# The pair of buffers in the router's place goes from the first to the fourth chunk of the first expert tile

## The chip, the cores and the metric

The kernel runs on one core of one Trainium2 chip, as one launch. The metric is the device time of that launch in microseconds; lower is better. The names of the engines are those of the profile: PE (TensorE, matrix multiply), PEld (its weight loads), DVE (VectorE), ACT (ScalarE), POOL (GpSimd), SP (the queue that issues most transfers).

## The reference

Three stages follow each other on 2304 tokens of 512 features.

```python
# 1: linear attention, 4 x 8 heads, 576 positions, 64 features per head
q_p, k_p = phi(q), phi(k)             # exp(+-(x @ w_phi - max|.|)), 256 features
attn = (q_p @ (k_p.T @ v)) / (q_p @ sum(k_p) + 1e-6)
# 2: a dense two-layer block on x [2304, 512]
h = x @ w_in                          # [2304, 2048]
x = np.maximum(0.01 * h, h) @ w_out   # [2304, 512]
# 3: each token goes to the one of 8 experts with the largest cosine logit
expert_idx = np.argmax(xn @ en.T / tau, axis=1)
for e in range(8):
    mask = expert_idx == e
    h = np.maximum(x[mask] @ w1[e], 0.0)          # w1[e] [512, 1024]
    out[mask] = gate_w[mask, None] * (h @ w2[e])  # w2[e] [1024, 512]
```

## The kernel before, in words

**Dense block.** Tokens go in 9 blocks of 256. The dense block's hidden features go in 16 chunks; the weights of a chunk are a tile `W` of high and low float32r parts. A first pass over the blocks uses chunks 0 to 7, a second pass (the loop `for j in range(NBLK)`) chunks 8 to 15, which lie in `ring_b`, a pool of eight such tiles. In the second pass `mm1(j, c)` (L344 to L346) forms a chunk of the hidden layer in a PSUM tile `h`; ACT and DVE make the leaky ReLU of it (L349, L351); ACT and POOL split it into `gg` (L353, L355); `mm2(j, c)` (L366) multiplies it by the second weight matrix, two chunks behind. `y_half_b(j)` then adds the two passes (L606), stores the block, and for blocks 0 to 7 takes the product of each token with each of the 8 expert embeddings on DVE (L615, 16 operations per block, all reading the tile `enb`).

**Expert tiles.** The tokens are sorted into tiles of 128 with one expert each; 23 tiles are always run. The list of the first five is made from the first 12 token tiles while the dense block still runs. A tile needs four weight chunks of [128, 2048] from `ew`: chunks 0 and 1 are the halves of w1, chunks 2 and 3 the halves of w2. POOL gathers chunk c into `raw[c]`; `split(c)` makes a high part `whi` (ACT, L921) and a low part `wlo` (DVE, L922), each in two operations over 1024 columns. The pair (`whi`, `wlo`) of each chunk stays where `first_split(c)` put it for the rest of the kernel; later tiles split into the same pair, and skip that if the expert is the same (branches, L932 and L935).

**Where the pairs lie.** `ring_c` has two tiles of [128, 2048] and opens, for the last block, in the place of the pool `lg`, which holds `enb`: what is written there first waits for the last L615 of block 7. `ring_b` gives its eight tiles in turn: the first pair has the place of `W` for dense chunks 8 and 9, the second of 10 and 11, the third of 12 and 13, each to be had after the last `mm2` that reads them.

**Work around the change.** PE's order is written out by hand there (`manual_schedule`), and ACT's too in the first two steps: `up(i, nh)` (12 matmuls with chunk nh, L978 to L982, into a PSUM tile that shares the two buffers of `h`), `hT` (4 transposes, L992, copied out by ACT L995 and DVE L996), `down(i, nh)` (12 matmuls with chunk 2 + nh, L1008 to L1012), `xT` (transposes of the next tile's tokens, L881, copied by L884 and L885). The transposes share a ring of two PSUM buffers `ps_t`. In `step(0)` the order is `up(0,0)`, then `ends()` (the last 12 matmuls of `mm2` of block 8), `hT(0,0)`, `up(0,1)`, `xT(1)`, `hT(0,1)`; in `step(1)` it is `up(1,0)`, `down(0,0)` and so on. All queues run in order. The order on DVE is a scheduler's.

Of the kernel before, what the change touches and what calls it, by code (L numbers as in the profile page):

```python
# [66 lines left out]
def tile_attention_moe_router_experts(ctx, tc, qT, kT, va, w_phi, moew, emb, embT, tau, ew, out):  # L67
# [382 lines left out]
    for j in range(NBLK):  # L450
# [15 lines left out]
        if j == NBLK - 1:  # L466
# [3 lines left out]
            ring_b = ctx.enter_context(tc.tile_pool(name="ring_b", bufs=8, side="left", reuse_waits="tile"))  # L470
# [428 lines left out]
    def load_w(i, c):  # L899
        if i == 0 or i >= N_PLAIN:  # L900
            load_rows(i, c)
            return
        if i not in need:
            need[i] = nc.values_load(
                lists[i][2], engines=[mybir.EngineType.Pool], min_val=0, max_val=4 * NE
            )
        with tc.If(need[i] < NE):
            load_rows(i, c)
# [8 lines left out]
    def split(c):  # L917
        hi, lo = pairs[c]
        for h in range(2):
            hs_ = slice(h * 1024, (h + 1) * 1024)  # L920
            nc.scalar.copy(out=hi[:, hs_], in_=raw[c][:, hs_])  # L921
            nc.vector.tensor_sub(lo[:, hs_], raw[c][:, hs_], hi[:, hs_].bitcast(F32))  # L922

    def first_split(c):
        pool = ring_c if c == 0 else ring_b
        pairs[c] = tuple(pool.tile([P, 2048], F32R, tag="W", name=n) for n in ("whi", "wlo"))
        split(c)
        load_w(1, c)
# [11 lines left out]
    for j in range(NBLK):  # L940
# [3 lines left out]
        if last:  # L944
            lg_cm.__exit__(None, None, None)
            ring_c = ctx.enter_context(tc.tile_pool(name="ring_c", bufs=2, side="right", reuse_waits="tile"))
# [142 lines left out]
    for c in range(4):  # L1089
        first_split(c)  # L1090
# [62 lines left out]
```

## Time and profile before

| | before |
|---|---|
| time, median of 3 runs (lowest to highest) | 927.18 us (926.13 to 929.4) |
| the profiled execution's own time | 925.01 us |
| span of that execution in the profile | 923.3 us |
| PE busy | 881.8 us, 96% of the span |
| DVE, ACT, POOL busy | 60%, 49%, 24% |
| mean granted TensorE clock | 0.984 of full |

The times inside the profile count from the span's start; 1.7 us of the profiled execution's time lie outside the span. A clock of 1.00 in the profile's rows is the upper of TensorE's two levels (2.4 GHz), 0.50 the lower (1.2 GHz). A row of the timeline gives start, duration, engine, line, operation, output and inputs, a count, and in square brackets the idle time ahead of it with what ended it.

### The profile page before, as it was taken

The page shows a single profiled execution, that of the slowest core. Times are in us where ns is not written, and L with a number is a line of the kernel's source. Part 1 is how long each engine was busy: PE and PEld are TensorE (multiplying, and loading weights), DVE is VectorE, ACT ScalarE, POOL GpSimd, SP SyncE. Part 2 cuts the span into 40 slices and gives each one's busy share as a digit, 9 for nine tenths or more (in the row PEclk, how much of TensorE's full clock was granted, in tenths as well). Part 3 has the DMA queues.
Part 4 walks back from the last instruction along what each step waited for, and adds up shares of the span by engine and source line. Part 5 has one row for each costly group of instructions (what it writes and reads, how often), then busy time and mean ns, then how long its engine had stood idle before and what let it go on. Part 6 is the DMA issues. An engine that isn't in the chain of part 4 may idle for free. (4 is left out here: it accounts for less than half of the span.)

```text
span 923.3 us, 18721 instructions
## 1 busy us (share of the span) xinstructions
PE 881.8 (96%) x7104; PEld 757.1 (82%) x7104; DVE 553.2 (60%) x1276; ACT 450.2 (49%) x904; POOL 225.3 (24%) x219
## 2 busy tenths in 40 slices
PE   8979999999999999899999999959999999999994
PEld 6768888889898888788888888838888888888883
DVE  6775557484765554748888899863422761113572
ACT  6965556484745654743333332523423862224571
POOL 2430113031111330033233333501113431113321
PEclk9989999999999999999999999979999999999998
DMA  8873423142130211943222221601014941114570
GB/s 280 290 239 99 133 75 127 50 123 103 48 107 24 104 69 61 324 166 112 86 103 92 98 89 65 240 23 36 28 49 149 351 150 47 41 41 168 183 265 31
DMA packets 42613, 112.36 MB, mean 122 GB/s; under 512 B 4558, under 2 KB 23118, under 8 KB 36496
## 3 DMA queue, kind: packets, MB, share of 16 engines
q1 hardware_dynamic: 33424, 61.48, 20.1%
q0 software_dynamic: 9008, 49.55, 15.4%
q8 instruction: 57, 0.93, 0.4%
q14 instruction: 44, 0.36, 0.1%
q10 hardware_dynamic: 80, 0.03, 0.0%
HBM read 87.45 MB, written 24.90 MB: 122 GB/s over the span
## 5 line engine op out<-in xcount | busy, mean ns | idle before, releaser
L366 PE MATMUL y<-W,gg 128*128 128x512 f32 x864 | 230.0, 400 | 1.0 <-ACT gg L353 1.0
L366 PEld LDWEIGHTS y<-W,gg 128*128 128x128 f32 x864 | 153.0, 189 | 29.0 <-ACT gg L353 1.4
L344 PE MATMUL h<-xb,W 128*128 128x256 f32 x576 | 164.3, 288 | 5.2 <-DVE g L351 3.3
L345 PE MATMUL h<-xb,W 128*128 128x256 f32 x576 | 162.7, 283 | 1.9 <-DVE xb L294 1.6
L346 PE MATMUL h<-xb,W 128*128 128x256 f32 x576 | 162.1, 283 | 0.0
L344 PEld LDWEIGHTS h<-xb,W 128*128 128x128 f32 x576 | 108.1, 189 | 13.3 <-DVE g L351 4.7
L345 PEld LDWEIGHTS h<-xb,W 128*128 128x128 f32 x576 | 108.5, 188 | 7.7 <-DVE xb L294 2.2
L252 POOL PARTITION_ALL_REDUCE qmx<-pr x28 | 56.4, 2016 | 221.6 <-ACT pr L234 218.0
L346 PEld LDWEIGHTS h<-xb,W 128*128 128x128 f32 x576 | 108.5, 189 | 1.6 <-issue 0.2
L353 ACT CAST gg<-g 128x256 fp32r<-128x256 f32 x144 | 57.5, 406 | 96.2 <-DVE g L351 87.5
L615 DVE CUSTOM_DVE_ANT_0 jk<-ys,enb 128x512 f32<-128x512 f32 x128 | 102.5, 801 | 2.0
L349 ACT ACTIVATE t<-h 128x256 f32<-128x256 f32 x144 | 54.5, 382 | 88.4 <-PE h L346 87.7
L351 DVE TENSOR_TENSOR g<-h,t 128x256 f32<-128x256 f32 x144 | 60.1, 420 | 53.4 <-ACT t L349 50.2
L355 POOL TENSOR_TENSOR gg<-g,gg 128x256 fp32r<-128x256 f32 x72 | 59.0, 823 | 134.5 <-ACT gg L353 117.7
L922 DVE TENSOR_TENSOR wlo<-raw,whi 128x1024 fp32r<-128x1024 f32 x56 | 68.1, 1255 | 36.0 <-ACT whi L921 30.3
L996 DVE TENSOR_TENSOR h<-htp,h 128x512 fp32r<-128x512 f32 x46 | 31.7, 689 | 92.9 <-ACTq L935 74.4
L978 PE MATMUL hps<-whi,xt 128*128 128x512 f32 x184 | 77.3, 420 | 9.9 <-ACT whi L921 9.8
L1008 PE MATMUL yo<-whi,h 128*128 128x512 f32 x184 | 74.7, 406 | 0.0
L979 PE MATMUL hps<-wlo,xt 128*128 128x512 f32 x184 | 73.7, 400 | 0.5 <-DVE wlo L922 0.5
L1009 PE MATMUL yo<-wlo,h 128*128 128x512 f32 x184 | 72.6, 395 | 0.0
L921 ACT CAST whi<-raw 128x1024 fp32r<-128x1024 f32 x56 | 55.9, 1047 | 34.2 <-PE hps L982 13.0
L985 ACT ACTIVATE hs<-hps 128x512 f32<-128x512 f32 x46 | 27.4, 595 | 71.3 <-PE hps L982 64.8
(239 smaller groups left out, 1600.0 us busy)
## 6 DMA issues: line engine op xcount, KB each, us to landing
wst<-in_moew_dram SPq DMA_DIRECT2D x32, 512.0 KB, 5.3
qraw<-in_q_dram SPq DMA_DIRECT2D x36, 256.0 KB, 3.0
xs_d<-xb SPq DMA_DIRECT2D x9, 1024.0 KB, 5.4
xb<-xs_d POOLq DMA_DIRECT2D x9, 1024.0 KB, 5.2
kraw<-in_k_dram SPq DMA_DIRECT2D x16, 288.0 KB, 3.3
yp_d<-yt SPq DMA_DIRECT2D x9, 512.0 KB, 3.7
yt<-yp_d SPq DMA_DIRECT2D x9, 512.0 KB, 3.8
y_d<-ys SPq DMA_DIRECT2D x18, 256.0 KB, 2.1
```

The costliest lines, as they stand in the source:

```text
L344: nc.tensor.matmul(hp, w[:, 0, ks], x[:, 0, k, :], start=(k == 0), stop=False)
L345: nc.tensor.matmul(hp, w[:, 0, ks], x[:, 1, k, :], start=False, stop=False)
L346: marks["mm1"] = nc.tensor.matmul(hp, w[:, 1, ks], x[:, 0, k, :], start=False, stop=(k == 3))
L351: nc.vector.tensor_tensor(out=g, in0=hp, in1=t, op=ALU.max)
L355: eng.tensor_sub(gg[:, 1, :], g, gg[:, 0, :].bitcast(F32))
L366: nc.tensor.matmul(yps[j][t], gg[:, a, ts], w[:, b, DM:2 * DM], start=(c0 == 0 and a == 0 and b == 0), stop=(c0 == NCH - 1 and a == 1),)
L615: nc.vector.tensor_tensor_reduce(out=jk2, in0=ys, in1=enb[:, e, :], scale=1.0, scalar=0.0, op0=ALU.mult, op1=ALU.add, accum_out=lgr[:, t, ...
L922: nc.vector.tensor_sub(lo[:, hs_], raw[c][:, hs_], hi[:, hs_].bitcast(F32))
L978: nc.tensor.matmul(ps, x[:, 0, k], hi[:, ks], start=(k == 0), stop=False)
L979: nc.tensor.matmul(ps, x[:, 0, k], lo[:, ks], start=False, stop=False)
L1008: nc.tensor.matmul(yacc[i], h2[:, 0, k], hi[:, w0], start=(nh == 0 and k == 0), stop=False)
L1009: nc.tensor.matmul(yacc[i], h2[:, 0, k], lo[:, w0], start=False, stop=False)
```

## The change

One number decides which chunk's pair comes out of `ring_c`.

```diff
     def first_split(c):
-        pool = ring_c if c == 0 else ring_b
+        pool = ring_c if c == 3 else ring_b
         pairs[c] = tuple(pool.tile([P, 2048], F32R, tag="W", name=n) for n in ("whi", "wlo"))
         split(c)
         load_w(1, c)
```

The four calls still come in the order c = 0, 1, 2, 3. Before, chunk 0 took `ring_c` and chunks 1, 2, 3 the first, second and third pair of `ring_b`; now chunks 0, 1, 2 take those three pairs and chunk 3 takes `ring_c`. No instruction is added or left out but branches of the control flow. The order moves on ACT, DVE and PE.

On ACT, around the last two `gg` of the dense block (`gg_8075`, `gg_8101`) and the first result of `up`, `hs_8179`; `raw0` to `raw3` are the chunks' raw weights, `whi_8110` the high part of chunk 0. Before:

```order
L353 CAST gg_8101<-g_8099 128x256 [waits DVE_49]
L907 UNCONDITIONAL_BRANCH
L921 CAST whi_8110<-raw0_5447 128x1024 [waits DMAHW1_49,DMASW1_49,DVE_49]
L921 CAST whi_8110<-raw0_5447 128x1024
L907 UNCONDITIONAL_BRANCH
L985 ACTIVATE hs_8179<-hps_8166 128x512 [waits PE_49,Pool_49]
```

Now the row after `gg_8101` is `hs_8179`, and the pair of casts that wait for DVE, now of chunk 3 (`raw3`), stands further on, between the two row sums of squares of block 8 (L609) and ahead of the copies of `hT(0,0)` and `up(0,1)` (`h2_8238`, `hs_8254`):

```order
L609 ACTIVATE jk_8226,sst_5362<-ys_8223 128x512 [waits DVE_49]
L921 CAST whi_8150<-raw3_5450 128x1024 [waits DMAHW1_49,DMASW4_49,DVE_49]
L921 CAST whi_8150<-raw3_5450 128x1024
L609 ACTIVATE jk_8231,sst_5362<-ys_8228 128x512 [waits DVE_49,Activation_49]
L995 CAST h2_8238<-htp_8233 128x512 [waits PE_49]
L985 ACTIVATE hs_8254<-hps_8241 128x512 [waits PE_49,Pool_49]
```

The casts of chunks 0, 1 and 2 stand where those of chunks 1, 2 and 3 stood.

On DVE, the stretch after the last product with the embeddings (`jk2_7880`, the 16th L615 of block 7). Before:

```order
L615 ISA jk2_7880,lgr_7839<-ys_7861,enb_5361 128x512 [waits DVE_49]
L615 ISA lgr_7839 128x1
L639 TENSOR_TENSOR lg_5363<-lgr_7839,esc_5436 128x16 [waits DVE_49]
L652 TENSOR_REDUCE mx_7883<-lg_5363 128x2 [waits DVE_49]
L654 TENSOR_TENSOR wt_7885<-lg_5363,mx_7883 128x16 [waits DVE_49]
L655 TENSOR_TENSOR wt_7885<-wt_7885,w8_5392 128x16 [waits DVE_49]
L657 TENSOR_REDUCE m2_7888<-wt_7885 128x2 [waits DVE_49]
L922 TENSOR_TENSOR wlo_8111<-raw0_5447,whi_8110 128x1024 [waits DMASW1_49,Activation_49]
```

Now, from the second L606 of block 8 on (`ys_8228`); the first L606 stands two products earlier, and a register load and a skipped branch (L932, L935) four products earlier:

```order
L606 TENSOR_TENSOR ys_8228<-y_7973,yt2_7627 128x512 [waits DMAHW3_49,DVE_49,PE_49]
L639 TENSOR_TENSOR lg_5363<-lgr_7839,esc_5436 128x16
L652 TENSOR_REDUCE mx_7883<-lg_5363 128x2 [waits DVE_49]
L654 TENSOR_TENSOR wt_7885<-lg_5363,mx_7883 128x16 [waits DVE_49]
L922 TENSOR_TENSOR wlo_8151<-raw3_5450,whi_8150 128x1024 [waits DMASW4_49,Activation_49]
L655 TENSOR_TENSOR wt_7885<-wt_7885,w8_5392 128x16 [waits DVE_49]
L935 COMPARE_AND_BRANCH
```

Behind this branch, whose body (a split for the next tile) is skipped where the expert stays, follow:

```order
L922 TENSOR_TENSOR wlo_8151<-raw3_5450,whi_8150 128x1024 [waits Activation_49]
L657 TENSOR_REDUCE m2_7888<-wt_7885 128x2 [waits DVE_49]
L996 TENSOR_TENSOR h2_8238<-htp_8233,h2_8238 128x512 [waits Activation_49]
L907 UNCONDITIONAL_BRANCH
L658 TENSOR_TENSOR oh_5364<-wt_7885,m2_7888 128x16 [waits DVE_49]
```

So both halves of the low part of chunk 3 now stand ahead of the copy of `hT(0,0)` (`h2_8238`). On PE the order named above stays; only four small matmuls of block 7's ranks (L664, L665) move from the middle of `up(0,0)` into `up(1,0)`. PE's first matmul of `up(0,0)` waited for ACT and now waits for DVE.

## Rows read from the trace of the kernel before

**Rows 1.** The page, 40 slices: busy tenths of PE, and its granted clock.

```profile
PE   8979999999999999899999999959999999999994
...
PEclk9989999999999999999999999979999999999998
```

**Rows 2.** Waits of PE, 586 to 660 us: total, times, longest.

```profile
PE hps L978 <- ACT whi L921: 9.8, 1, 9.8
```

**Rows 3.** Timeline of PE from the last `mm2` in the loop to `down(0,0)`.

```profile
599.16 1.56 PE L366 MATMUL y<-W,gg 128*128 128x512 f32 x6
610.57 0.80 PE L978 MATMUL hps<-whi,xt 128*128 128x512 f32 x1 [9.85 <-ACT whi L921]
...
620.25 0.63 PE L992 MATMUL htp<-ident,hs 128*128 128x128 f32 x4
620.64 0.48 PE L978 MATMUL hps<-whi,xt 128*128 128x512 f32 x1
...
623.53 0.60 PE L881 MATMUL xtp<-ident,xgt 128*128 128x128 f32 x4
624.44 0.66 PE L992 MATMUL htp<-ident,hs 128*128 128x128 f32 x4 [0.31 <-ACTq L935]
...
628.79 0.48 PE L1008 MATMUL yo<-whi,h 128*128 128x512 f32 x1
```

**Rows 4.** Timeline of ACT, 609 to 629 us.

```profile
609.48 1.99 ACT L921 CAST whi<-raw 128x1024 fp32r<-128x1024 f32 x2 [6.19 <-DVE lgr L615]
...
620.44 0.63 ACT L609 ACTIVATE jk<-ys 128x512 f32<-128x512 f32 x1 [2.55 <-DVE ys L606]
...
621.20 0.63 ACT L609 ACTIVATE jk<-ys 128x512 f32<-128x512 f32 x1
...
625.13 0.59 ACT L995 CAST h<-htp 128x512 fp32r<-128x512 f32 x1
628.26 0.60 ACT L985 ACTIVATE hs<-hps 128x512 f32<-128x512 f32 x1 [2.54 <-PE hps L982]
```

**Rows 5.** Timeline of DVE, 601 to 623 us.

```profile
601.50 0.41 DVE L351 TENSOR_TENSOR g<-h,t 128x256 f32<-128x256 f32 x1
...
602.77 3.12 DVE L922 TENSOR_TENSOR wlo<-raw,whi 128x1024 fp32r<-128x1024 f32 x2
605.82 0.68 DVE L615 CUSTOM_DVE_ANT_0 jk<-ys,enb 128x512 f32<-128x512 f32 x1
...
606.54 0.69 DVE L615 CUSTOM_DVE_ANT_0 jk<-ys,enb 128x512 f32<-128x512 f32 x1
...
609.48 0.17 DVE L639 TENSOR_TENSOR lg<-lgr,esc 128x16 f32<-128x16 f32 x1
609.68 0.17 DVE L652 TENSOR_REDUCE mx<-lg 128x2 f32<-128x16 f32 x1
...
610.55 1.23 DVE L922 TENSOR_TENSOR wlo<-raw,whi 128x1024 fp32r<-128x1024 f32 x1
...
619.71 1.39 DVE L606 TENSOR_TENSOR ys<-y,yt 128x512 f32<-128x512 f32 x2 [6.44 <-PE y L366]
...
622.47 0.69 DVE L996 TENSOR_TENSOR h<-htp,h 128x512 fp32r<-128x512 f32 x1
```

**Rows 6.** DVE's queue at the branches: duration in ns (min/median/max).

```profile
L932 DVEq TENSOR_LOAD <-esk x4: 306/434/577, 613.1 to 654.4; - x4
```

**Rows 7.** Stretches: busy time of five engines, then granted clock, DMA share, GB/s.

```profile
604.00:605.00 1.00, 0.00 (x0) 0.00 (x0) 1.00 (x2) 0.00 (x0) 0.81 (x1) 0.62 0.00 0
...
617.00:618.00 1.00, 1.00 (x4) 0.81 (x3) 0.00 (x0) 0.60 (x1) 0.00 (x0) 0.55 0.00 0
```

**Rows 8.** Other waits of PE and, last, the stretch in which the clock rose.

```profile
373.44 0.38 PE L344 MATMUL h<-xb,W 128*128 128x256 f32 x1 [2.78 <-DVE g L351]
...
64.92 2.07 PE L366 MATMUL y<-W,gg 128*128 128x512 f32 x4 [1.03 <-ACT gg L353]
...
68.00:69.00 1.00, 1.00 (x9) 1.00 (x8) 0.57 (x1) 0.00 (x0) 0.72 (x1) 0.82 0.92 283
```

## Prediction

> **What bounds the kernel now.** I read the page's slices first: PE stands at 7 tenths or more everywhere but in the 27th of the 40 slices (600 to 623 us), which has 5, and in the last; between these two every slice stands at 9 [rows 1]. What makes PE start earlier behind that slice is therefore won at the end, as long as nothing else comes late there. The view of PE's waits then gives that hole one cause: 9.8 us until ACT's cast of a high part (L921) [rows 2]. PE's timeline shows the place: the last six `mm2` of the loop begin at 599.16 and take 1.56, PE is empty from 600.72 to 610.57, then `up(0,0)` begins [rows 3]. ACT stands idle 6.19 us ahead of that cast, from 603.29, until DVE's last product with the embeddings [rows 4]; DVE itself has no hole, it works through six products (a pitch of 0.72) [rows 5]. So `up(0,0)` waits for chunk 0, chunk 0 for the place of `enb`, and that for DVE's backlog.
>
> The hole costs more than its length. The clock falls to the lower level within 604 to 605 and is back within 617 to 618; 0.62 and 0.55 as means of these two stretches put the edges at 604.2 and 617.9 [rows 7]. From 610.57 to 617.9 PE works 7.3 us at half speed, which loses 3.7 us.
>
> **What the change takes away.** Chunk 0 now has the place in the queues that chunk 1 had. DVE's queue tells when PE can begin: `up(0,0)` writes the PSUM buffer that dense chunk 14 leaves free, and its L351 runs from 601.50 to 601.91 [rows 5]. The low parts of chunks 0 and 1 stand ahead of this L351 in DVE's order, so they are done by then. `up(0,0)` begins at about 601.95, after a wait of 1.2 us in the place of 9.85. I take the clock to stay up there: a wait of 2.78 us that ended at 373.44 [rows 8] lies in the 17th slice, whose clock digit is 9 [rows 1].
>
> **Where the next wait comes.** I walk PE's order with durations at the upper clock. `up` from its first matmul to the next kind takes 623.53 - 620.64 = 2.89 [rows 3], so `up(0,0)` ends at 604.84. `ends()` is again 12 matmuls of 512 columns, 2.89: 607.73; its `gg` tiles were cast before ACT went idle at 603.29 [rows 4]. `hT(0,0)` takes 0.39 (620.25 to 620.64): 608.12. `up(0,1)`: 611.01. `xT(1)` 0.60: 611.61 [rows 3]. The next is `hT(0,1)`, and here the moved pair bites: it needs `hs(0,1)` from ACT and the PSUM buffer of `hT(0,0)`, which is free only after ACT's L995 and DVE's L996. Both now stand behind the casts and the low parts of chunk 3, and these behind the last L615.
>
> DVE: the low parts of the third pair end at 602.77 + 3.12 = 605.89, one L615 follows to 606.5 [rows 5]. Then comes the register load with the skipped branch, which was covered before by DVE's wait for PE and is not now: 0.31 to 0.58 for the load [rows 6]; I take 0.6 with the jump. Two L615 (0.72 each) to 608.55; L606, half of 1.39, to 609.25 (PE's sums for it are done by 607.73); two L615 to 610.7. The last L615 is thus later than the 609.4 of before. L606 to 611.4, three small operations at a pitch of 0.2 to 612.0. First low half, 1.23: 613.2; one small operation and the jump, 0.3: 613.5; second low half: 614.7; a small one 0.2; L996 0.69: 615.6 [rows 5].
>
> ACT: casts of chunk 3 from 610.7, 1.99: 612.7; L609, 0.76 from one to the next: 613.45; L995 0.59: 614.05; `hs(0,1)` 0.60: 614.65 [rows 4]. DVE is the later one. `hT(0,1)` begins at 615.6, and PE has waited 615.6 - 611.6 = 4.0 us.
>
> **The clock.** In the old hole the clock fell 3.5 us after PE went empty (604.2 - 600.72), so I expect a fall in this wait of 4.0 too, at its very end or just behind. What follows at half speed has no row of its own. From below it is nothing (the 2.78 us wait). From above it is the 3.7 of the old hole. Between them stands a fall near 61: PE took up steady work at 64.92 and the clock was back at about 68.4, 3.4 us at half speed, 1.7 lost [rows 8]. I take 2.7, the middle of 1.7 and 3.7, since the new wait lies nearer to the old hole than to 2.78.
>
> The Trainium skill (TensorE: Matmul & The Clock Gate, section "HAM oscillation — how this bites in real kernels") describes a kernel in which waits between bursts of matmuls throttle the clock again each time, so that each burst starts cold. [...] This trace agrees for the long wait at 600 and shows no fall for the one at 373.
>
> **The sum.** From `hT(0,1)` to `down(0,0)` PE took 628.79 - 624.44 = 4.35 at full clock [rows 3]. `down(0,0)` then begins at 615.6 + 4.35 + 2.7 = 622.65 in the place of 628.79: 6.1 us earlier. Behind it the slices are full, the order is the same, and the lists for later tiles are made from sums that come still earlier, so I carry 6.1 to the end. Chunk 3 itself is needed first by `down(0,1)`, some 8 us behind `down(0,0)`, and is ready by 614.7: no wait. Against the profiled execution's own 925.01 that gives 918.9; it lies 2.2 below the median of 927.18, and on the median the change makes 921.1. I say 921.0.
>
> **Rivals.**
> 1. *The new wait, but no fall of the clock* (or one that ends at once): 8.8 us won, with a chain 0.7 shorter 9.5: 917.7 to 918.4. For it: 2.78 us passed. Against it: 3.5 was enough at 600. Chance 0.18.
> 2. *The change doesn't do what it says at first:* `up(0,0)` stays bound to DVE until the third pair's low parts too, since DVE's order has them close by. Start at 605.9, a wait of 5.2, the clock low from 604.2; 7.3 us of slow work as before loses 3.7, so `ends()` is through at 605.9 + 5.8 + 3.7 = 615.4, its first half, for which L606 waits, about 0.7 earlier. From that L606 to L996 the chain takes 615.6 - 608.55 = 7.05: `hT(0,1)` at 621.75, `down(0,0)` at 626.1, 2.7 won: 924.5. Against it: the buffer it waits for is chunk 14's, ahead of those low parts. Chance 0.08.
> 3. *The clock falls after the first wait as well,* as it does near 61 around waits of about 1 us: 3.7 lost before `ends()`, whose first half is through near 610.7 and moves the chain by 2.2; `hT(0,1)` at 617.8, `down(0,0)` at 622.1, with the second fall 624.8: 4.0 won, 923.2. Against it: the single wait of 2.78. Chance 0.07. [...]
> 4. *Slower:* the jumps on DVE and ACT, until now hidden in waits, cost more than their rows, while every copy of the first tile stands behind them. With 2.7 for the clock it turns slower when `hT(0,1)` begins after 615.6 + 6.1 = 621.7. Two jumps stand on DVE's chain, so each would have to cost over 3 us more than summed; at 4 us more each `hT(0,1)` begins at 623.6 and the kernel takes 929. Against it: the dearest register load is 577 ns [rows 6]. Chance 0.05.
>
> **Numbers.** The forecast has 0.62: 3 to 8 us won, that is 919 to 924.2, from the clock's loss between 0.8 and 3.7 and a chain up to 2 us longer. The range reaches down past rival 1, and up to rival 2: 917.3 to 924.7; what is left out is rival 4, and the edges of 2 and of the spread of the three runs. A change of under 0.3% (2.8 us) can't be told from none here. Faster: the forecast, rivals 1 and 3, with some of the forecast's upper edge given to "same": 0.84. Same: rival 2 and that edge, 0.11. Slower: 0.05.
>
> **What would show it.** Right: PE begins L978 near 602 with a wait near 1.2 put down to L351; a wait near 4 us ahead of `hT(0,1)` (L992), put down to L996 or ACT; L921 of chunk 3 begins right at the end of the last L615, near 610.7; granted clock 1.00 from 602 to 611 and 0.50 for some microseconds after 615; `down(0,0)` near 622.6; no other new wait behind it. Wrong: a wait of 5 us at `up(0,0)`; a wait ahead of `hT(0,1)` far from 4 us; a clock that stays up, or stays down past 623; or a gain at `down(0,0)` that is given back at the switch to later experts.

## The result, and the profile after

| | before | after |
|---|---|---|
| time, median of 4 runs each (lowest to highest) | 927.39 us (926.13 to 929.4) | 920.16 us (919.15 to 920.74) |
| ratio after/before, 95% interval | | 0.9919 [0.9897, 0.9941] |
| the profiled execution's own time, span | 925.01, 923.3 us | 920.74, 918.9 us |
| mean granted TensorE clock | 0.984 | 0.990 |

The change made the kernel 0.8% faster, 7.2 us between the medians. In the page after, the slice with 5 tenths of PE is gone; the 27th slice of the clock row, 7 tenths before [rows 1], is 9:

```profile
PE   7879999999999999899999999989999999999994
PEclk9989999999999999999999999999999999999998
```

The view of PE's waits for 586 to 660 us, whose largest row was 9.8 us put down to ACT's L921 [rows 2], now has two smaller ones (in total, times, longest):

```profile
PE htp L992 <- DVE oh L658: 3.3, 1, 3.3
PE hps L978 <- DVE g L351: 1.2, 1, 1.2
```

The timeline of PE after, where [rows 3] stood before:

```profile
601.24 1.56 PE L366 MATMUL y<-W,gg 128*128 128x512 f32 x6
604.03 0.50 PE L978 MATMUL hps<-whi,xt 128*128 128x512 f32 x1 [1.23 <-DVE g L351]
...
606.93 2.96 PE L366 MATMUL y<-W,gg 128*128 128x512 f32 x12
609.73 0.60 PE L992 MATMUL htp<-ident,hs 128*128 128x128 f32 x4
...
612.97 0.60 PE L881 MATMUL xtp<-ident,xgt 128*128 128x128 f32 x4
616.87 1.09 PE L992 MATMUL htp<-ident,hs 128*128 128x128 f32 x4 [3.29 <-DVE oh L658]
...
622.55 0.48 PE L1008 MATMUL yo<-whi,h 128*128 128x512 f32 x1
```

All that comes ahead of this stretch ran 2.1 us later in this execution (601.24 against 599.16 for the last six `mm2` of the loop), so starts are compared as distances from that row. `down(0,0)` stands 622.55 - 601.24 = 21.3 us behind it; before it was 628.79 - 599.16 = 29.6. The stretch won 8.3 us. The wait of 3.29 us is put down to L658, which stands right behind L996 on DVE; the transposes read nothing of L658, and L996 ends only 0.08 us ahead of it.

The stretches after (five engines, then the granted clock) show the one fall of the clock that is left in this part, from 616.5 to 619.9 by the means of its two edge rows; those of before are [rows 7]:

```profile
604.00:605.00 1.00, 0.97 (x4) 0.83 (x5) 1.00 (x4) 0.45 (x2) 0.51 (x1) 1.00 0.00 0
...
616.00:617.00 1.00, 0.13 (x1) 0.17 (x2) 1.00 (x5) 0.49 (x1) 0.00 (x0) 0.73 0.79 193
617.00:618.00 1.00, 1.00 (x5) 1.00 (x6) 0.63 (x3) 0.01 (x1) 0.00 (x0) 0.50 0.20 78
618.00:619.00 1.00, 1.00 (x3) 0.74 (x3) 0.39 (x1) 0.58 (x1) 0.00 (x0) 0.50 0.00 0
619.00:620.00 1.00, 1.00 (x4) 0.77 (x3) 0.30 (x1) 0.00 (x0) 0.00 (x0) 0.56 0.06 16
```

On DVE the chain towards the new wait reads like this after (before: [rows 5]); ACT's casts of chunk 3 run from 612.21, once the last product is through:

```profile
608.79 0.69 DVE L615 CUSTOM_DVE_ANT_0 jk<-ys,enb 128x512 f32<-128x512 f32 x1 [0.18 <-DVEq L935]
...
611.47 0.69 DVE L615 CUSTOM_DVE_ANT_0 jk<-ys,enb 128x512 f32<-128x512 f32 x1
...
613.37 1.22 DVE L922 TENSOR_TENSOR wlo<-raw,whi 128x1024 fp32r<-128x1024 f32 x1
...
614.82 1.23 DVE L922 TENSOR_TENSOR wlo<-raw,whi 128x1024 fp32r<-128x1024 f32 x1
...
616.04 0.68 DVE L996 TENSOR_TENSOR h<-htp,h 128x512 fp32r<-128x512 f32 x1
```

```profile
612.21 1.99 ACT L921 CAST whi<-raw 128x1024 fp32r<-128x1024 f32 x2 [0.62 <-DVE lgr L615]
614.11 0.63 ACT L609 ACTIVATE jk<-ys 128x512 f32<-128x512 f32 x1
...
615.20 0.60 ACT L985 ACTIVATE hs<-hps 128x512 f32<-128x512 f32 x1
```

**What was given back.** From that last `mm2` to the span's end it is 923.3 - 599.16 = 324.14 us before and 918.9 - 601.24 = 317.66 after: 6.5 won of the 8.3. One later wait is new, at a switch of experts:

```profile
730.93 0.66 PE L992 MATMUL htp<-ident,hs 128*128 128x128 f32 x4 [0.64 <-ACT hs L985]
```

The outputs `o` (L1017) of the two tiles around it come 13.39 + 12.52 us apart, before 12.82 + 11.97: 1.1 us. The remaining 0.7 is no wait: each later tile took 12.52 in the place of 12.47 us. This goes with the place of the pairs in all profiles of this document: the usual later tile takes 12.45 to 12.50 us where chunk 0 has the embeddings' place (before, e5, e7) and 12.50 to 12.53 where chunk 3 has it (after, e1, e4, e6, e8 to e11). So it comes with the change; what makes a tile longer there is open.

### The profile page after: what moved, and what is told of

It reads as the page before. It is cut to its first block, busy times and chain, and to the rows that moved or that the text cites. A ratio compares the mean times of both kernels' runs of the same rounds, so it can differ in the third digit from the quotient of the medians.

```text
span 918.9 us, 18718 instructions
## 1 busy us (share of the span) xinstructions
PE 880.8 (96%) x7104; PEld 756.7 (82%) x7104; DVE 552.9 (60%) x1276; ACT 450.4 (49%) x904; POOL 226.7 (25%) x219
## 5 line engine op out<-in xcount | busy, mean ns | idle before, releaser
L615 DVE CUSTOM_DVE_ANT_0 jk<-ys,enb 128x512 f32<-128x512 f32 x128 | 102.6, 801 | 2.1 <-DVEq L935 0.2
L351 DVE TENSOR_TENSOR g<-h,t 128x256 f32<-128x256 f32 x144 | 60.1, 420 | 53.6 <-ACT t L349 49.4
L996 DVE TENSOR_TENSOR h<-htp,h 128x512 fp32r<-128x512 f32 x46 | 31.7, 689 | 90.1 <-ACTq L935 74.8
L979 PE MATMUL hps<-wlo,xt 128*128 128x512 f32 x184 | 73.4, 399 | 0.0
L921 ACT CAST whi<-raw 128x1024 fp32r<-128x1024 f32 x56 | 55.9, 1046 | 29.4 <-PE hps L982 13.5
```

The source lines that it names most:

```text
L351: nc.vector.tensor_tensor(out=g, in0=hp, in1=t, op=ALU.max)
L615: nc.vector.tensor_tensor_reduce(out=jk2, in0=ys, in1=enb[:, e, :], scale=1.0, scalar=0.0, op0=ALU.mult, op1=ALU.add, accum_out=lgr[:, t, ...
L979: nc.tensor.matmul(ps, x[:, 0, k], lo[:, ks], start=False, stop=False)
```

## Experiments

Ratios are to runs of the kernel before on the same chip: median 926.41 us for e1 to e4, 926.97 for e5 to e8, 925.89 for e9 to e11. "Distance" is that from the last six `mm2` of the loop to `down(0,0)`: 29.6 us before, 21.3 after.

**e1, the changed kernel again**, as the yardstick of e2 to e4.

> The changed kernel once more, beside the kernels of this group, as their yardstick. Theory (the hole of 9.85 us at the first up and the slow clock behind it go, a wait of 3.3 us at hT(0,1) with a short fall of the clock comes): 920.2 us, ratio 0.992; PE waits 1.2 us at L978 and 3.3 us at L992. In its first profile some 1.1 us were lost again near 730 us, at the switch of experts (a wait of 0.64 us at L992 there). If that loss belongs to the kernel, it is there again; if it was chance, this run goes without it.

921.04 us, 0.9948 [0.9929, 0.9967]. Waits of 1.24 and 3.29 us, distance 621.56 - 600.06 = 21.5. The late wait near 730 is there again, with 0.4.

**e2, the place for chunk 2 instead of 3.**

```diff
-        pool = ring_c if c == 3 else ring_b
+        pool = ring_c if c == 2 else ring_b
```

> The pair in the embeddings' place goes to chunk 2 (needed first by down(0,0)), chunks 0, 1, 3 take the ring. Theory: what counts is only that the chunk which has to wait for the embeddings isn't due on PE before about 617; down(0,0) starts at 622.5, so chunk 2 is in time as well, PE's order and its waits (1.2 and 3.3 us) stay: 920.2, within 0.2% of the changed kernel. Rival (the chunk in this place must be the one due last, or its place in memory matters): slower by 2 us or more than the changed kernel, with a wait at down(0,0).

919.03 us, 0.9926 [0.9910, 0.9943]; waits of 1.22 and 3.31, distance 619.46 - 598.06 = 21.4. Which half of w2 comes last makes no difference to the distance, which fits a wait for the copies that stand behind the late split, and not for the chunk itself; e4 asks this directly. The times of e1 and e2 can't be told apart.

**e3, the place for chunk 1,** which `up(0,1)` needs.

```diff
-        pool = ring_c if c == 3 else ring_b
+        pool = ring_c if c == 1 else ring_b
```

> The pair in the embeddings' place goes to chunk 1 (needed by up(0,1), just behind hT(0,0)). Theory: up(0,0) and ends() run as early as in the changed kernel, but up(0,1) waits 3 to 4 us for the cast and again for the two low halves, and xT(1), hT(0,1) come behind it: hT(0,1) 1.5 to 2.5 us later than in the changed kernel, more work at the lower clock: 922 to 924. Rival (all of the gain comes from freeing chunk 0): as fast as the changed kernel, 920. Rival (any wait of up on this place costs what it cost before): 927.

921.93 us, 0.9950 [0.9932, 0.9967]; the distance is 625.37 - 601.66 = 23.7, 2.4 us more than after. PE's timeline has the waits at `up(0,1)` for the chunk itself, both parts of it:

```profile
613.75 0.50 PE L978 MATMUL hps<-whi,xt 128*128 128x512 f32 x1 [2.97 <-ACT whi L921]
...
615.08 0.79 PE L979 MATMUL hps<-wlo,xt 128*128 128x512 f32 x1 [0.83 <-DVE wlo L922]
```

The clock is at the lower level from near 614.3 to near 621.2. So, at `down(0,0)`, the late pair costs the more the earlier its chunk is needed: 29.6 with chunk 0, 23.7 with chunk 1, 21.4 with either half of w2. The times do not show the 2.4 us: e3's ratio is that of e1. In the traces the span ends 318.4 us behind the last `mm2` in e3 and 317.7 and 317.6 in after and e1, so most of the 2.4 is gone by the end.

**e4, the split of chunk 3 issued one step later.** The place stays; only the split leaves the queues ahead of the copies of `hT(0,0)`.

```diff
     def hooks(i, n):
+        if (i, n) == (1, 1):
+            first_split(3)
         if (i, n) in steps:
...
-    for c in range(4):
+    for c in range(3):
         first_split(c)
```

> As the changed kernel, but the split of chunk 3 is written into step (1,1), so that its casts on ACT and its low parts on DVE stand behind the copies of hT(0,0), up(0,1) and hT(0,1). Theory (the new wait at hT(0,1) is made by the order of the queues: the copies stand behind the split of chunk 3): the wait falls from 3.3 to about 1.6 us, the clock doesn't fall, hT(0,1) to down(0,0) takes 4.4 in the place of 5.7: 3 us faster than the changed kernel, 917. Rival (the wait comes from the sums of block 8, L606 and L609, which stay where they are, or from the backlog of L615): the wait stays above 3 us and the time at 920.

918.05 us, 0.9906 [0.9886, 0.9927]. The wait of 3.3 us has shrunk to two short ones, and the clock stays up:

```profile
616.02 0.17 PE L664 MATMUL prk<-oh,upper 128*128 128x8 bf16 x1 [0.67 <-DVE oh L658]
...
616.88 0.63 PE L992 MATMUL htp<-ident,hs 128*128 128x128 f32 x4 [0.65 <-ACTq L935]
```

```profile
616.00:617.00 1.00, 0.33 (x4) 0.27 (x4) 0.92 (x3) 0.89 (x3) 0.58 (x1) 1.00 0.26 94
617.00:618.00 1.00, 1.00 (x8) 0.90 (x8) 0.76 (x2) 0.66 (x2) 0.00 (x0) 1.00 0.64 139
```

The distance is 621.05 - 603.01 = 18.0, 3.3 less than after: 2.0 less waiting and 1.3 of slow clock. That the split ahead of the copies makes the second wait is shown by this. No wait near 730 us here, and the span ends 313.6 us behind the last `mm2`, 4.1 less than after.

**e5, the hole of before filled.** 38 matmuls of 512 columns, whose sums nobody reads, are put on PE behind the last `mm2` of the loop in the kernel before.

```diff
-J_PE = 8
+J_PE = 8; N_FILL = 38
...
-                nc.tensor.matmul(
+                marks["mm2"] = nc.tensor.matmul(
...
+    def filler(i):
+        if i:
+            return
+        ft = ps_r.tile([P, 512], F32, tag="pp", name="fill")
+        with tc.issue_after(marks["mm2"].ins):
+            for n in range(N_FILL):
+                nc.tensor.matmul(ft, xt[0][:, 0, n % 4], pairs[1][0][:, 0:512], start=True, stop=True)
...
-            up(i, 0)
+            filler(i); up(i, 0)
```

> The kernel before with 38 more matmuls of 512 columns on PE (8.9 us at the upper clock, their sums are read by nobody) in its hole of 9.85 us, between the last mm2 of the loop and up(0,0). Theory (the hole costs its length, and by itself the slow clock behind it 3.7 us): up(0,0) starts when it did, the clock stays at the upper level, down(0,0) comes 3 to 3.7 us earlier: ratio about 0.9965. Rival (the clock's fall is a sign of the hole and costs nothing of its own, since PE waits there for others too): the same time as before, or slower by what the fillers overrun.

925.52 us, 0.9991 [0.9971, 1.0010]. PE's timeline:

```profile
602.73 9.03 PE L1007 MATMUL fill<-whi,xt 128*128 128x512 f32 x38
612.74 0.49 PE L978 MATMUL hps<-whi,xt 128*128 128x512 f32 x1 [0.97 <-ACT whi L921]
...
614.00 0.50 PE L979 MATMUL hps<-wlo,xt 128*128 128x512 f32 x1 [0.77 <-DVE wlo L922]
```

The clock stays at 1.00 all through. `up(0,0)` begins no earlier (612.74 - 601.34 = 11.4 behind the last `mm2`, as before), so the wait for chunk 0 is not PE's doing. From there to `down(0,0)`, which begins at 628.36, it takes 15.6 us in the place of 628.79 - 610.57 = 18.2: the slow clock had cost 2.6 us net. The 3.7 of the prediction counted all of the 7.3 us as work at half speed. But the first 1.26 us, to the first L979, are the same in both: what a faster first matmul saves is waited for the low part (0.77 in the place of 0.46). And behind them matmuls of 512 columns follow each other at 0.43 us in the slow clock and at 0.23 here, not quite double.

The expected ratio of 0.9965 was missed: it lies outside the interval, and 2.6 us (0.9972) lie at its edge. The trace alone carries the 2.6; in it the span ends 321.8 us behind the last `mm2`, in the place of 324.1, so 2.4 of them come through.

**e6, the second wait filled.** Twelve such matmuls, in a PSUM tile of the same tag `pp`, behind `xT(1)` in the changed kernel; nobody reads their sums.

```diff
...
-            xT(i + 1)
+            xT(i + 1); filler(i)
```

> The changed kernel with 12 more matmuls of 512 columns on PE (2.8 us, read by nobody) in its wait of 3.3 us ahead of hT(0,1). Theory: hT(0,1) starts when it did, the clock does not fall, hT(0,1) to down(0,0) takes 4.4 in the place of 5.7 us: 1.3 us faster than the changed kernel, of which the times can tell little, so the trace decides. Rival (the clock's fall behind this wait costs nothing): 5.7 us stay, or hT(0,1) moves later.

923.47 us, 0.9943 [0.9921, 0.9965], and it missed its purpose. The added matmuls waited themselves, and the clock fell ahead of most of them:

```profile
617.83 4.61 PE L999 MATMUL fill<-whi,xt 128*128 128x512 f32 x12 [2.32 <-ACTq L935]
```

`hT(0,1)` came 3.5 us later than in the changed kernel (622.27 - 603.17 = 19.1 in the place of 15.6 behind the last `mm2`). It says nothing on the price of the clock; why they waited is not settled. e9 asks the question in another way.

**e7 and e8, the logits of block 7 on PE instead of DVE,** in the kernel before and in the changed one. DVE then has no products with `enb` behind it at this place.

```diff
-J_PE = 8
+J_PE = 7
```

> The kernel before with the logits of block 7 on PE (transposes and 8 small matmuls, as block 8 has them) in the place of its 16 products on DVE, so that the embeddings are read last in block 6. Theory (the hole is DVE's backlog of products holding the place that chunk 0 waits for): the hole goes, PE has 3 us more to do, the wait ahead of hT(0,1) stays below 2 us: 917 to 920. Rival (the hole comes from the raw weights' transfer, or from ACT): the hole stays near 10 us, and the time at 927 or above.

> The changed kernel with the logits of block 7 on PE. Theory (the change is worth only what the backlog in front of the embeddings' place costs): with the backlog gone it makes no difference which chunk has that place: within 0.3% of the kernel before with the same alteration. Rival (the change is worth something by itself, through the order of the splits or the place in memory): 0.6% or more faster than that one.

e7: 927.02 us, 0.9999 [0.9983, 1.0015]; e8: 929.87, 1.0034 [1.0015, 1.0053]. In both PE goes into `up(0,0)` without a wait, so DVE's products were what held the place. But nothing is won, where 917 to 920 was expected of e7: the schedule changes ahead of it, and new waits arise, in e7

```profile
587.09 0.58 PE L344 MATMUL h<-xb,W 128*128 128x256 f32 x1 [3.23 <-DVE g L351]
...
591.01 1.11 PE L881 MATMUL xtp<-ident,xgt 128*128 128x128 f32 x4 [0.98 <-DMA xgt<-y_d,egi]
```

and in e8

```profile
594.56 1.11 PE L881 MATMUL xtp<-ident,xgt 128*128 128x128 f32 x4 [6.33 <-DMA xgt<-y_d,egi]
```

each with a fall of the clock behind it: in e7 to the lower level from near 586 to near 603. Against a common row ahead of these waits (an `mm2` pair at 583.15 and 586.09), `down(0,0)` stands 45.8 us behind in e7 and 46.4 in e8, which is 0.6 of the 2.9 us between the medians. The later execution is already 2.9 us behind at that common row; what made it so stays open. From the last six `mm2` of the loop (610.27 and 613.77), behind those waits, `down(0,0)` stands 18.7 and 18.8 us behind: in this stretch it makes no difference any more which chunk has the place. The times, 0.35% apart, just miss the 0.3% expected of e8.

**e9, the work ahead of the second wait lengthened.** Nine matmuls at the head of `up(0,1)` in the changed kernel, into its own PSUM tile and overwritten.

```diff
-        ps = ps_m.tile([P, 512], F32, tag="h", name="hps")
+        ps = ps_m.tile([P, 512], F32, tag="h", name="hps"); [nc.tensor.matmul(ps, x[:, 0, n % 4], hi[:, 0:512], start=True, stop=True) for n in range(9 if (i, nh) == (0, 1) else 0)]
```

> Nine matmuls of 512 columns, whose sums are overwritten and read by nobody, are added at the head of up(0,1), the work ahead of the new wait; about 2.1 us. If the slow work behind hT(0,1) comes from the wait of 3.3 us ahead of it: the wait shrinks to about 1.2 us, hT(0,1) begins at the same distance from the last mm2 of the loop (15.6 us), the granted clock stays at 1.00, hT(0,1) to down(0,0) takes 4.35 us in the place of 5.7, and down(0,0) stands about 20.0 us behind that mm2 in the place of 21.3 to 21.5: about 1.3 us less, which the times cannot tell from the changed kernel. If the slow work has another cause (the clock would fall there anyway): the clock falls as before, 21.3 to 21.5. If the added work delays the copies of the first tile: hT(0,1) later than 16 us behind that mm2.

917.82 us, 0.9910 [0.9880, 0.9939]. In this execution PE had waited 1.46 us for a transfer at 597, and not at `up(0,0)`, so `ends()` is the better anchor than the last `mm2`:

```profile
607.31 2.96 PE L366 MATMUL y<-W,gg 128*128 128x512 f32 x12
...
610.46 2.35 PE L975 MATMUL hps<-whi,xt 128*128 128x512 f32 x9
...
617.01 0.63 PE L992 MATMUL htp<-ident,hs 128*128 128x128 f32 x4 [0.96 <-ACT xt L884]
...
621.30 0.48 PE L1008 MATMUL yo<-whi,h 128*128 128x512 f32 x1
```

```profile
617.00:618.00 1.00, 0.99 (x7) 0.92 (x8) 0.96 (x4) 0.33 (x2) 0.28 (x1) 1.00 0.10 20
618.00:619.00 1.00, 1.00 (x6) 0.82 (x5) 0.74 (x2) 0.26 (x1) 0.00 (x0) 1.00 0.81 229
```

`hT(0,1)` stands 9.7 us behind `ends()` (after: 9.9), the clock stays up, and from `hT(0,1)` to `down(0,0)` it takes 4.29 us, in the place of 5.68. So 2.35 us of useless work on PE did not delay `hT(0,1)` and saved 1.4 us behind it: with PE at work in most of the gap, no slow work followed. That is one execution; in the times it can't be seen, since the median of e9 is that of e11 below.

**e10 and e11, e4 and the changed kernel once more,** side by side with e9.

> The version whose first split of chunk 3 is issued one step later, once more, in more rounds, beside the changed kernel. If it truly saves both the rest of the wait and the slow clock behind it (3.3 us in the trace): 0.3 to 0.4% below the changed kernel of the same call, down(0,0) about 18 us behind the last mm2 of the loop. If what the first run showed was the spread of times: the two intervals cover each other.

> The changed kernel unaltered, as the yardstick of this call: two waits of 1.2 and 3.3 us, down(0,0) 21.3 to 21.5 us behind the last mm2 of the loop. If the late wait ahead of hT near 730 us (0.64 and 0.4 us in its first two profiles) belongs to the kernel, it is there a third time; if it was chance, it is not.

e10: 915.93 us, 0.9886 [0.9858, 0.9914], distance 619.37 - 601.28 = 18.1, the clock up. e11: 917.82, 0.9922 [0.9894, 0.9949], waits of 1.26 and 3.29, distance 621.94 - 600.42 = 21.5. The intervals of e4 and e1 lie apart, those of e10 and e11 overlap; by the ratios the later split is worth 3.9 and 3.3 us, and at `down(0,0)` the traces of the two pairs have 3.5 and 3.4. The span ends 313.6 us behind the last `mm2` in e4 and e10, and 317.4 to 317.7 in the three profiles of the changed kernel. It is the best version found. The change itself is worth 7.2, 5.4 and 8.1 us between the medians of the three sets of runs (the result, e1, e11). e11 has no row for a wait near 730; its two tiles there take 12.82 + 12.53 us.

## Why the prediction was right, step by step

**`up(0,0)` is bound to chunk 14's buffer.** Right: the wait is 1.23 us, put down to L351, as foreseen; rival 2 (bound to the third pair's low parts) is out. The change moved the wait only as far as the buffer of `h`.

**The clock stays up there.** Right: 1.00 from 604 to 605. Rival 3 is out. The prediction had taken this from the 2.78 us wait at 373. The digit that it read there could not show it: a slice is 23 us long, and a fall of 3.4 us leaves its digit at 9, as the slice of after with the fall at 616 has. The stretches of 1 us of before do show 1.00 there, but the same wait is followed by a fall in other executions (last section), so that bound stood on luck.

The Trainium skill (TensorE: Matmul & The Clock Gate, section "HAM oscillation — how this bites in real kernels") describes a kernel whose waits for transfers, each longer than the burst of matmuls ahead of it, throttle the clock, so that each burst starts cold. The wait of 3.29 us here, with 0.50 behind it, agrees, though it is one for copies; a wait as short as 1.23 us is not what the section describes, so the 1.00 behind that one does not speak against it. The wait of 3.44 us in e7 does: it passed at 1.00 (last section).

**The new wait ahead of `hT(0,1)`.** The mechanism is right, and e4 shows it: take the split out of the queues there, and the wait shrinks to 0.67 and 0.65. The size was 4.0 and is 3.29. Counted from the last `mm2`, `hT(0,1)` was to begin at 615.6 - 599.16 = 16.4 us and began at 15.6. Half of the 0.8 is the register load and the branch on DVE, summed at 0.6 and seen at 0.18; the rest is spread over the chain. Rival 4 lived on these jumps costing more; they cost less.

**The clock behind it.** It falls, as expected, near the wait's end (616.5 in after), so rival 1 is out; it does so in all four profiles with this wait (after, e1, e2, e11). But it costs 5.68 - 4.35 = 1.3 us (1.5 in e1 and e11) where 2.7 was summed. This is the term that was mis-sized most. The upper of the two neighbours it was taken from was too dear: the old hole cost 2.6 net and not 3.7 (e5). There the clock had gone down 6.4 us before PE took up work, and stayed down for another 7.3; here it was down for about 3 us of work. The row near 61, 1.7 lost, was the better neighbour than the middle that I took. The lower one, nothing, stood on one execution.

**The carry to the end.** 6.1 us were summed and 8.3 won at `down(0,0)`, by these two terms. That 8.3 comes through whole was wrong: 6.5 reach the end in the trace, and 7.2 between the medians. The text had named the switch to later experts as the place where a gain might be given back, but gave it no price; by its own list, a gain given back there was a sign of being wrong. From `down(0,0)` to the span's end it is 295.9 to 296.4 us in the three profiles of the changed kernel and 294.5 to 294.8 in before, e5 and e7, so 1.1 to 1.8 us are given back. Longer later tiles are 0.7 to 1.0 of it, and the rest lies at the switch, where the two tiles take 25.4 to 25.9 us in the place of 24.8 to 25.3. The late wait shows in two of three profiles of this kernel (0.64 and 0.4 us, none in e11) and in none of e4, e9 and e10, so it is not all of it. `hs` stands there on ACT behind casts for the next expert; that this order makes the wait was only argued. So the forecast of 921.0 is nearer to 920.16 than its terms deserve: too small a gain in the stretch, with no loss behind it.

## What to carry to other kernels

A buffer that comes free late should go to the consumer that is needed last, and its producer should stand in the queues behind everything that is needed sooner: the first half of this was the change (8.3 us at `down(0,0)`), the second half is e4 (3.3 more). When a wait of PE is cut, look at what the moved instructions now stand ahead of on in-order queues, and price the clock from rows of several executions, since one of them may have passed a wait by luck. Useless work in a gap was free in e9, and not in e6, where it had to wait itself.

## What was not expected of the hardware

A fall of the clock is not one price. After the hole of 9.85 us it lost 3.7 us of PE's time by the windows, and 2.6 net (e5); after the wait of 3.29 us it lost 1.3 to 1.5 (after, e1, e11; against e9, 1.4); after one of 3.23 in e7 the clock was down from 586.0 to 603.1, with PE at work in most of that.

The length of a wait does not tell whether a fall comes either. One wait for L351, near 373 us, stands in every profile of this document. The clock stayed at 1.00 behind it in before, after, e2, e7 and e11, with waits of 2.78, 2.77, 2.54, 3.44 and 3.04 us, and fell in e3, e4 and e9, with 2.66, 2.96 and 2.90, as behind the waits of 3.41 to 3.94 in the others. In e7 and e3:

```profile
372.79 0.39 PE L344 MATMUL h<-xb,W 128*128 128x256 f32 x1 [3.44 <-DVE g L351]
...
374.00:375.00 1.00, 1.00 (x10) 1.00 (x10) 1.00 (x3) 0.73 (x3) 0.00 (x0) 1.00 1.01 410
```

```profile
374.29 0.38 PE L344 MATMUL h<-xb,W 128*128 128x256 f32 x1 [2.66 <-DVE g L351]
...
376.00:377.00 1.00, 1.00 (x7) 1.00 (x7) 0.99 (x4) 0.57 (x3) 0.00 (x0) 0.50 1.05 406
```

What decides between these is open. Waits of 1.2 us ahead of `up(0,0)`, and of 0.67 and 0.65 with three small matmuls between (e4, e10), lost nothing.

The skipped branch on DVE cost 0.18 us between two products, where the register load beside it shows 0.31 to 0.58 [rows 6]. And whole executions shift by several microseconds ahead of the change: the last `mm2` of the loop began between 598.06 (e2) and 603.17 us (e6) in kernels whose program ahead of it computes the same. The traces differ ahead of that row, with one fall of the clock in e2 and four in e4 (603.01), but two in e6, so the falls alone do not explain the shifts. A gain must be read from distances between rows.
